# A fused retention and gated MLP kernel: states and cross products in 64-wide TensorE tiles, with the head halves of two of four pairs swapped

## The chip, the core and the metric

The kernel runs on one core of one Trainium2 chip. The metric is the time of one execution on the device in microseconds, as the median of several runs. The core has five engines that this text names as the profile does: PE (TensorE, the matrix unit), DVE (VectorE), ACT (ScalarE), POOL (GpSimd) and SP (SyncE, which issues the DMAs here). PE reads its operands from SBUF and writes into PSUM, which has eight banks of 512 fp32 columns; DVE and ACT carry results from PSUM back to SBUF. A PE matmul has a stationary operand (the weights, brought in by a separate weight load, "PEld" in the profile) and a moving operand.

## The reference

Eight batches, eight heads, 576 positions, head size 64. Each head does retention: scores decayed by a power of a head's gamma, and no softmax. The result is laid out as 4608 tokens of 512 features and goes through an MLP with a gate.

```
scores = q @ k.T / sqrt(64)
ret    = scores * gamma[h] ** (i - j)   for j <= i, else 0
attn   = ret @ v                        # (8, 8, 576, 64)
x      = attn.transpose(0, 2, 1, 3).reshape(4608, 512)
h      = x @ w_in                       # 512 x 2048
g      = h * sigmoid(beta * h)
out    = g @ w_out                      # 2048 x 512, fp32
```

## The kernel before, in words

**Retention by chunks.** Since the decay is a power of the distance, it is split into a factor on q (`gq`) and one on v (`gv`). The first 512 positions of a batch are four chunks of 128 keys (`c` = 0 to 3); the last 64 positions of two batches together make a "tail" block. `seq` lists all of them in order, and every helper takes an index `i` into it. The eight heads are four pairs `p`, the two heads `j` of a pair lying on the two halves of 64 partitions. For a chunk:

- `a_sc` (L320) makes scores: for each pair and each head a matmul of 64 rows of weights (`kT`), so that the two heads of a pair use the upper and the lower half of the array, each into a PSUM bank of its own. DVE multiplies them by the causal mask into `R`.
- `a_O` (L375) multiplies `R` by v: weights of 128 rows and 64 columns, so that the two heads of a pair write the two halves of the output's partitions.
- `a_st` (L404) adds k^T v of the chunk to a running state in PSUM: four matmuls, one per pair, each 128 x 128 with 128 moving columns. Of each 128 x 128 result only the two diagonal 64 x 64 blocks are wanted; two ACT copies (L419) carry them to a tile `sbd` (or `end`, after the last chunk), whose other two blocks were set to zero at the start (L155).
- `a_cross` (L356) adds what earlier chunks give: q times the state before this chunk, four matmuls per chunk (L372), each with a block-diagonal 128 x 128 `sbd` as weights and 128 moving columns, into the same PSUM bank as `a_O`'s. Tails use `ends` with 64 moving columns (L369).
- `a_x` (L390) copies the finished block from PSUM to `xT`, the transposed activations.

**The MLP.** `up` (L424) multiplies four slices `ko` of `w_in` (128 rows each, one per head pair) by `xT` with 512 moving columns and lets ACT apply the gate (L433) into `gT`; `down` (L457) multiplies `gT` by `w_out` (L464), and a copy and a DMA carry the result out. Both run in bf16 with 512 moving columns.

**The order of work** is written out by hand. `fill` is a list of up and down steps of all blocks, one after the other. `merged` (L484) emits them in order and, at numbered places, what the `streams` hold: loads, casts, transposes and the retention of the next batch. A batch from number 2 on has at one place `first` (L596: state of chunk 0, scores of chunks 0 and 1), two steps later the state of chunk 1, at a later place `first` again (state of chunk 2, scores of chunks 2 and 3), and five steps after that `outputs` (L601: all four `a_O`, the three crosses, the four copies, the state of chunk 3). Batches 0 and 1 are at the start and partly written out line by line (L498 to L593). Each engine runs its instructions in the order in which they are emitted.

**The start.** `w_in` arrives on SP's queue in seven pieces of columns (L165: six of 256 and one of 512) and is cast to bf16 by DVE and POOL (`cast_w_in`, L180), half of the 128-row slices each. Behind it come the four groups of `w_out`, into the same four staging buffers `wt`, and are cast and scaled by 1/beta (`cast_w_out`, L198): group 0 by DVE (three slices) and POOL (one), groups 1 to 3 by DVE and ACT. The first block's up steps run while the pieces arrive; its down steps start with the first two slices of `w_out` (`down_rows`, L551). Behind `w_out` the q, k and v of batch 1 are loaded.

Of the kernel before, what the change touches and what calls it, by code (L numbers as in the profile page):

```python
# [19 lines left out]
def kernel(  # L20
# [10 lines left out]
    nc = tc.nc  # L31
# [139 lines left out]
    def load_w_in(g):  # L171
        f0, fn = pieces[g]
        if f0 % 512 == 0:
            whole[0] = stage.tile([P, KO, 512], F32, name="wt", tag="wt", bufs=4)
        t = whole[0][:, :, f0 % 512:f0 % 512 + fn]
        for w in (slice(0, 2), slice(2, KO)) if g in (0, 1, NP - 1) else (slice(0, KO),):
            nc.sync.dma_start(t[:, w], w_in_r[:, w, f0:f0 + fn])  # L177
        wts[g] = t

    def cast_w_in(g, kos=range(KO)):  # L180
        t = wts[g]
        f0, fn = pieces[g]
        for ko in kos:
            on_pool = ko < 2 if g == 0 else ko % 2
            e = nc.gpsimd if on_pool else nc.vector
            if fn > 256 and ko == 2:
                for x in range(0, fn, 256):
                    for o, eng in ((2, nc.vector), (3, nc.gpsimd)):
                        eng.tensor_copy(w_in_sb[:, o, f0 + x:f0 + x + 256], t[:, o, x:x + 256])
            elif fn == 256 or ko < 2:  # L190
                e.tensor_copy(w_in_sb[:, ko, f0:f0 + fn], t[:, ko])  # L191

    def load_w_out(g):
        t = stage.tile([P, KO, d_model], F32, name="wt", tag="wt", bufs=4)
# [3 lines left out]
    def cast_w_out(g):  # L198
        t = wts.pop(NP + g)
        for i in range(KO):  # L200
            fo = g * KO + i
            if i == KO - 1 and g == 0:
                nc.gpsimd.tensor_tensor(w_out_sb[:, fo, :], t[:, i], rbeta_sb[:, fo:fo + 1].to_broadcast([P, d_model]), ALU.mult)
            elif i == KO - 1:
                nc.scalar.activation(w_out_sb[:, fo, :], t[:, i], ACT.Copy, scale=rbeta_sb[:, fo:fo + 1])
            else:
                nc.vector.tensor_scalar(w_out_sb[:, fo, :], t[:, i], rbeta_sb[:, fo:fo + 1], None, ALU.mult)  # L207
# [76 lines left out]
    def heads(t, p):  # L284
        return t[:, 2 * p:2 * p + 2, :].rearrange("p h d -> p (h d)")
# [63 lines left out]
    def O_of(i, p):  # L349
        Os = live[i]["O"]  # L350
        return Os[p // 2][:, p % 2] if split(i) else Os[0][:, p]

    def opens(i, p):
        return p == 0 or split(i) and p == 2

    def a_cross(i, first):  # L356

        b, c = seq[i]
        if first:
            new_O(i)  # L360
        if c == 0 and b is not None:
            return
        for p in range(HP):
            rhs, view = q_cols(i, slice(0, P), p)
            O = O_of(i, p)
            if b is None:
                for x in range(2):
                    r = slice(x * TL, (x + 1) * TL)
                    nc.tensor.matmul(O[:, r], ends[(2 * c + x) % 4][:, p, :], rhs[:, r],  # L369
                                     start=False, stop=True, skip_group_check=True)  # L370
            else:
                nc.tensor.matmul(view(O), sbds[(c - 1) % NS][:, p, :], rhs,  # L372
                                 start=first and opens(i, p), stop=not first, skip_group_check=True)

    def a_O(i):  # L375

        b, c = seq[i]
        L = live[i]

        early = i < E  # L380
        if not early:
            new_O(i)
        R, vn = L["R"], L["vn"]
        crossed = b is None or c > 0
        for j, p in [(n // HP, n % HP) if early else (n % 2, n // 2) for n in range(H)]:
            nc.tensor.matmul(O_of(i, p)[j * D:(j + 1) * D], vn[:, 2 * p + j, :], R[:, j, p, :],  # L386
                             start=opens(i, p) and not (early and crossed), stop=early or not crossed,
                             skip_group_check=True)

# [14 lines left out]
    def a_st(i):  # L404

        b, c = seq[i]
        if b is None:
            return
        L = live[i]
        if c == 0:  # L410
            state_ps[b] = psum.tile([P, HP, P], F32, name="st", tag="st", bufs=1)
        st = state_ps[b]
        for p in range(HP):
            nc.tensor.matmul(st[:, p, :], heads(L["kn"], p), heads(L["vn"], p),  # L414
                             start=(c == 0 and p == 0), stop=True, skip_group_check=True)
        s = ends[b % 4] if c == CB - 1 else sbds[c % NS]
        for j in range(2):
            r = slice(j * D, (j + 1) * D)
            (nc.vector.tensor_copy if i == CB + 2 else nc.scalar.copy)(s[r, :, j * D:(j + 1) * D], st[r, :, j * D:(j + 1) * D])  # L419


    gts = {}
# [71 lines left out]
    def F(f, *a):  # L494
        return lambda: f(*a)
# [76 lines left out]
    def second(i):  # L572
        for f in (a_O, lambda j: a_cross(j, False), a_x):
# [32 lines left out]

    def pair_prep(i, at):
        b, c = seq[i]
# [18 lines left out]
    for n in range(1, B - 1):  # L627

        take = [i for i in todo if seq[i][0] == n + 1 or n == B - 2 or seq[i] == (None, 0) and n == CB - 1]
        todo = todo[len(take):]  # L630
        lo, hi = (base[n] + 17, base[n + 1] - 9.5) if n == 1 else (base[n] + 3, base[n + 1] - 8)
        at = [lo + x * (hi - lo) / (len(take) - 1) for x in range(len(take))]
        if len(take) == 2 and n > 1:
            at[1] -= 6
        for i, t in zip(take, at):
            st = pair_prep(i, t) + [(t, F(first, i))]
            if seq[i][0] is None:
                st.append((t + 5, F(second, i)))
# [37 lines left out]
```

## Time and profile before

| what | value |
|---|---|
| median of three runs | 307.72 us (307.54 to 307.96) |
| the profiled execution's own time | 308.28 us |
| its span, first to last instruction | 306.6 us |
| granted PE clock | 1.0 throughout |
| PE busy / weight loads busy | 298.1 us (97%) / 155.8 us (51%) |
| DVE / ACT / POOL busy | 105.8 (35%) / 141.2 (46%) / 99.5 us (32%) |
| PE, 0 to 21.0 us | 15.97 us busy |
| PE, 21.0 to 34.2 us | 12.87 of 13.2 us busy |
| PE, 34.2 to 248 us | busy without a gap worth naming |
| HBM traffic | 36.71 MB read, 9.44 MB written |

The profiled execution took 1.68 us more than its span, and 0.56 us more than the median. Busy time of PE counts a matmul from its start to its modelled end, and matmuls overlap, so "97% busy" says that PE was seldom without work, not that it ran at its peak: what a matmul costs is read from the distance between starts. The chain of work that ended last, one of the views, gives these distances in groups: a start, a length, an engine with its tile and line, and how many instructions.

### The profile page before, as it was taken

What the parts mean: (1) busy time and instruction counts of PE and PEld (TensorE: products, weight loads), DVE (VectorE), ACT (ScalarE), POOL (GpSimd) and SP (SyncE); (2) the same over time, 40 slices, a digit from 0 to 9 for tenths busy, and PEclk for the clock granted to TensorE, in tenths of its full rate; (3) what the DMA queues carried; (4) which work ended last, traced back from release to release, by engine and by line L of the source; (5) the groups of instructions that cost most, each with busy time, mean ns of one, the idle gap of its engine ahead of it and who ended that gap; (6) DMA issues with size and microseconds to landing.
All of it is one profiled execution on the core that took longest, in us unless ns stands there. A gap on an engine that the chain in (4) does not pass through costs nothing.

```text
span 306.6 us, 5337 instructions
## 1 busy us (share of the span) xinstructions
PE 298.1 (97%) x2145; PEld 155.8 (51%) x2145; DVE 105.8 (35%) x192; ACT 141.2 (46%) x249; POOL 99.5 (32%) x136
## 2 busy tenths in 40 slices
PE   7789999999999999999999999999999999999996
PEld 5544456855554454454554545454545444444444
DVE  7554466504730433234430623053414420010012
ACT  5567546783148313660286208710773047207700
POOL 4666117653743264354326032812330000000000
PEclk9999999999999999999999999999999999999999
DMA  8999999999999999999994499939980110031012
GB/s 211 218 335 379 382 239 255 231 193 236 177 276 179 238 270 222 216 263 187 186 258 77 106 223 259 169 88 206 203 126 2 71 68 0 23 79 36 0 68 71
DMA packets 128697, 53.84 MB, mean 176 GB/s; under 512 B 109968, under 2 KB 121632, under 8 KB 128672
## 3 DMA queue, kind: packets, MB, share of 16 engines
q1 hardware_dynamic: 128640, 53.49, 79.9%
q8 instruction: 17, 0.28, 0.4%
q14 instruction: 8, 0.07, 0.1%
q10 hardware_dynamic: 32, 0.01, 0.0%
HBM read 36.71 MB, written 9.44 MB: 151 GB/s over the span
## 4 chain that ended last, share of the span: by engine, by line
PE 88%; DMA 5%; SPq 4%; DVE 1%; POOL 0%; issue 0%; DVEq 0%
PE po L464 41%; PE ph L431 36%; DMA wt<-in_moe_w_out_dram 3%; SPq L95 3%; PE sc L330 3%; PE O L386 3%; DMA wt<-in_moe_w_in_dram 2%; PE st L414 2%; PE O L372 2%; SPq L177 1%; DVE w_out_sb L207 1%; PE O L369 0%; SPq L83 0%; PE T L304 0%; PE T L310 0%
## 5 line engine op out<-in xcount | busy, mean ns | idle before, releaser
L433 ACT ACTIVATE gT<-ph,beta_sb 128x512 bf16<-128x512 f32 (+1 forms) x152 | 99.1, 659 | 82.6 <-PE ph L431 82.2
L464 PE MATMUL po<-w_out_sb,gT 128*128 128x512 bf16 (+2 forms) x608 | 129.2, 368 | 0.4 <-DVE w_out_sb L207 0.4
L431 PE MATMUL ph<-xT,w_in_sb 128*128 128x512 bf16 (+1 forms) x608 | 127.4, 365 | 0.0
L431 PEld LDWEIGHTS <-w_in_sb 128*128 128x128 bf16 x608 | 58.2, 98 | 61.6 <-DVE w_in_sb L191 0.7
L464 PEld LDWEIGHTS <-gT 128*128 128x128 bf16 x608 | 57.1, 98 | 63.1 <-issue 0.6
L335 DVE TENSOR_TENSOR R<-sc,causal 128x512 bf16<-128x512 f32 x72 | 45.0, 684 | 78.2 <-PE sc L330 77.1
L471 DVE COPY ot<-po 128x512 f32<-128x512 f32 (+2 forms) x34 | 22.4, 659 | 85.0 <-PE po L464 84.9
L262 POOL TENSOR_TENSOR vn<-kvn,gv 128x512 bf16<-128x512 f32 x32 | 33.2, 1042 | 19.8 <-PE O L386 9.6
L280 POOL CAST kn<-kvn 128x512 bf16<-128x512 f32 x32 | 19.6, 615 | 44.1 <-DMA kvn<-in_k_dram 39.2
L254 POOL TENSOR_TENSOR qs<-qn,gq 128x512 bf16<-128x512 f32 x24 | 24.3, 1042 | 28.1 <-DMA qn<-in_q_dram 28.1
L419 ACT CAST sbd<-st 64x256 bf16<-64x256 f32 x46 | 16.7, 363 | 18.8 <-PE st L414 18.2
L402 DVE CAST xT<-O 128x512 bf16<-128x512 f32 x24 | 15.7, 687 | 16.5 <-PE O L386 9.1
L402 ACT CAST xT<-O 128x512 bf16<-128x512 f32 x10 | 5.9, 587 | 30.9 <-PE O L372 30.9
L414 PE MATMUL st<-vn,kn 128*128 128x128 bf16 x128 | 12.4, 219 | 0.1
L414 PEld LDWEIGHTS <-kn 128*128 128x128 bf16 x128 | 9.2, 98 | 4.7
L330 PE MATMUL sc<-qT,kT 64*128 64x128 bf16 x256 | 10.8, 218 | 0.7 <-ACT kT L311 0.6
L386 PEld LDWEIGHTS <-vn 128*64 128x64 bf16 x288 | 8.5, 109 | 4.5 <-issue 3.6
L386 PE MATMUL O<-R,vn 128*64 128x128 bf16 x288 | 10.8, 221 | 0.0
L269 POOL TENSOR_TENSOR kn<-tln,gq 128x512 bf16<-128x512 f32 x4 | 4.2, 1042 | 19.4 <-DMA tln<-in_q_dram 19.4
L330 PEld LDWEIGHTS <-kT 64*128 64x128 bf16 x288 | 8.2, 94 | 4.5 <-issue 1.7
L191 POOL CAST w_in_sb<-wt 128x256 bf16<-128x256 f32 (+1 forms) x13 | 6.3, 508 | 5.0 <-DMA wt<-in_moe_w_in_dram 5.0
L215 PE MATMUL ph<-warm 128*128 128x128 f32 (+1 forms) x24 | 6.6, 409 | 1.2 <-DVE warm L120 1.2
(62 smaller groups left out, 92.4 us busy)
## 6 DMA issues: line engine op xcount, KB each, us to landing
qn<-in_q_dram SPq DMA_DIRECT2D x16, 512.0 KB, 5.4
kvn<-in_k_dram SPq DMA_DIRECT2D x32, 256.0 KB, 5.2
kvn<-in_v_dram SPq DMA_DIRECT2D x32, 256.0 KB, 5.1
out_dram<-ot SPq DMA_DIRECT2D x31, 256.0 KB, 3.0
wt<-in_moe_w_out_dram SPq DMA_DIRECT2D x4, 1024.0 KB, 10.0
wt<-in_moe_w_in_dram SPq DMA_DIRECT2D x6, 512.0 KB, 8.5
out_dram<-ot SPq DMA_DIRECT2D x9, 128.0 KB, 2.4
wt<-in_moe_w_in_dram SPq DMA_DIRECT2D x4, 256.0 KB, 6.3
```

The costliest lines, as they stand in the source:

```text
L254: e.tensor_tensor(batch[b]["qs"][:, cs, hs], q_tiles[b][:, hs, cs].rearrange("p h i d -> p i h d"), gq[:, cs, hs].unsqueeze(3).to_broadcas ...
L262: nc.gpsimd.tensor_tensor(live[i]["vn"][:], kv_tiles.pop(i)[:, 1], gains(gv, c), ALU.mult)
L280: nc.gpsimd.tensor_copy(kn[:, c % 2], t[:, 0])
L330: nc.tensor.matmul(view(sc[j][:, p, :]), L["kT"][r, p, :], rhs, start=True, stop=True, skip_group_check=True)
L335: nc.vector.tensor_tensor(R[:, j], sc[j][:], m_b, ALU.mult)
L386: nc.tensor.matmul(O_of(i, p)[j * D:(j + 1) * D], vn[:, 2 * p + j, :], R[:, j, p, :], start=opens(i, p) and not (early and crossed), stop= ...
L402: (nc.scalar.copy if on_act else nc.vector.tensor_copy)(x, view(Os[0]))
L414: nc.tensor.matmul(st[:, p, :], heads(L["kn"], p), heads(L["vn"], p), start=(c == 0 and p == 0), stop=True, skip_group_check=True)
L431: nc.tensor.matmul(ph, w_in_sb[:, ko, fo * P:(fo + 1) * P], xts[m][:, ko, :, w], start=(ko == 0), stop=(ko == KO - 1))
L433: nc.scalar.activation(gts[m][:, fo, :, w], ph, ACT.Silu, scale=beta_sb[:, fo:fo + 1])
L464: nc.tensor.matmul(po[:, :nn], gT[:, fo, ms, :], w_out_sb[:, fo, n0:n0 + nn], start=(fo == 0), stop=(fo == FO - 1))
L471: (nc.scalar.copy if m == 0 else nc.vector.tensor_copy)(ot, po[:, :nn])
```

## The change

- **States.** For batches from number 2 on (`b >= QB`), `a_st` makes a state by eight matmuls instead of four: per head, weights of 128 rows and 64 columns, 64 moving columns, the two heads of a pair into the two halves of the partitions. The state lies dense in PSUM, 64 columns per pair, and after chunks 0 to 2 one ACT copy of 128 x 256 takes it to a new tile `sbq`; after chunk 3 two copies take it to `ends` as before.
- **Cross products.** For these batches `crosses` replaces `a_cross`: per chunk eight matmuls of 64 rows and 64 columns with 128 moving columns. They go in groups of four that use the four 64 x 64 quarters of the array: upper rows to left columns, lower rows to right columns, and for a pair with a number two higher the other two.
- **Swapped halves.** So that the second two of the four can write the other half of the partitions, the two heads of pairs 2 and 3 change places everywhere behind the scores: in `a_O` (all batches), in `ends` and `sbds` (ten blocks of 64 columns now, L152), in `xT`, and in the rows of `w_in` of slices 2 and 3.
- **Output tiles.** `a_O4` puts two chunks and two pairs into one PSUM bank instead of one chunk and four pairs; `x4` copies the four banks to `xT`, three by DVE and one by ACT.
- **Order.** The state of chunk 1 moves from two steps behind the first `first` to the beginning of the second; the state of chunk 2 moves from there to the beginning of `outputs`, in front of the 32 matmuls of `a_O4`, and the state of chunk 3 from the end of `outputs` to between `a_O4` and `crosses`. `a_O` of batch 0 takes the heads of a pair in turn.
- **Casts of w_in.** All pieces have 256 columns (eight pieces). POOL casts slices 0 and 1 of each; DVE casts slices 2 and 3, each in two copies of 64 partitions that change places. The last piece's cast and the load of the last `w_out` group are two steps later (10.1 and 10.2). Of `w_out` group 0, POOL casts two slices instead of one and DVE two instead of three.

```diff
-    sbds = [consts.tile([P, HP, P], BF16, name=f"sbd{i}") for i in range(NS)]
-    ends = [consts.tile([P, HP, P], BF16, name=f"end{i}") for i in range(4)]
+    sbds = [consts.tile([P, 10, D], BF16, name=f"sbd{i}") for i in range(1)]
+    ends = [consts.tile([P, 10, D], BF16, name=f"end{i}") for i in range(4)]
+    sbq = [consts.tile([P, HP, D], BF16, name=f"sbq{i}") for i in range(NS)]
     for s in sbds + ends:
         nc.vector.memset(s[:], 0.0)
+    sbds += ends[2:]
...
-    pieces = [(f, 256) for f in range(0, 1536, 256)] + [(f, 512) for f in range(1536, d_ff, 512)]
+    pieces = [(f, 256) for f in range(0, d_ff, 256)]
...
-        for w in (slice(0, 2), slice(2, KO)) if g in (0, 1, NP - 1) else (slice(0, KO),):
+        for w in (slice(0, 2), slice(2, KO)) if g < 2 else (slice(0, KO),):
...
-    def cast_w_in(g, kos=range(KO)):
+    def cast_w_in(g):
         t = wts[g]
         f0, fn = pieces[g]
-        for ko in kos:
-            on_pool = ko < 2 if g == 0 else ko % 2
-            e = nc.gpsimd if on_pool else nc.vector
...
+        for ko in range(2):
+            nc.gpsimd.tensor_copy(w_in_sb[:, ko, f0:f0 + fn], t[:, ko])
+        for ko in range(2, KO):
+            for hh in range(2):
+                nc.vector.tensor_copy(w_in_sb[hh * D:(hh + 1) * D, ko, f0:f0 + fn], t[(1 - hh) * D:(2 - hh) * D, ko])
...
-            if i == KO - 1 and g == 0:
+            if i % 2 and g == 0:
                 nc.gpsimd.tensor_tensor(w_out_sb[:, fo, :], t[:, i], rbeta_sb[:, fo:fo + 1].to_broadcast([P, d_model]), ALU.mult)
...
+    def block(s, p):
+        f = 2 * p
+        return s[:, f:f + 2].rearrange("k h d -> k (h d)")
...
-        for j, p in [(n // HP, n % HP) if early else (n % 2, n // 2) for n in range(H)]:
-            nc.tensor.matmul(O_of(i, p)[j * D:(j + 1) * D], vn[:, 2 * p + j, :], R[:, j, p, :],
+        for hh, p in [(n % 2, n // 2) for n in range(H)]:
+            j = hh ^ p // 2
+            nc.tensor.matmul(O_of(i, p)[hh * D:(hh + 1) * D], vn[:, 2 * p + j, :], R[:, j, p, :],
...
-        st = state_ps[b]
+        st, tiled = state_ps[b], b >= QB
         for p in range(HP):
-            nc.tensor.matmul(st[:, p, :], heads(L["kn"], p), heads(L["vn"], p),
-                             start=(c == 0 and p == 0), stop=True, skip_group_check=True)
+            if tiled:
+                for j in range(2):
+                    nc.tensor.matmul(st[j * D:(j + 1) * D, p, :D], L["kn"][:, 2 * p + j, :], L["vn"][:, 2 * p + j, :],
+                                     start=(c == 0 and p == 0), stop=True, skip_group_check=True)
+            else:
+                nc.tensor.matmul(st[:, p, :], heads(L["kn"], p), heads(L["vn"], p),
+                                 start=(c == 0 and p == 0), stop=True, skip_group_check=True)
+        if tiled and c < CB - 1:
+            nc.scalar.copy(sbq[c % NS][:], st[:, :, :D])
+            return
         s = ends[b % 4] if c == CB - 1 else sbds[c % NS]
...
+    def crosses(i):
+
+        for c in range(1, CB):
+            for p, x in [(p, x) for p in range(2) for x in range(4)]:
+                r, hh, p = slice(x % 2 * D, x % 2 * D + D), x % 2 ^ x // 2, p + x // 2 * 2
+                rhs, _ = q_cols(i + c, r, p)
+                nc.tensor.matmul(out4(i + c, p, hh), sbq[c - 1][r, p, :], rhs, start=False, stop=True, skip_group_check=True)
+
+    def out4(i, p, hh):
+
+        c = seq[i][1]
+        return live[i - c]["O4"][c // 2, p // 2][hh * D:(hh + 1) * D, p % 2, :, c % 2 * PC:(c % 2 + 1) * PC]
+
+    def a_O4(i):
...
+        if c % 2 == 0:
+            for u in range(2):
+                live[i - c]["O4"][c // 2, u] = psum.tile([P, 2, CB, 2 * PC], F32, name="O", tag="sc" if c else "O", bufs=2)
+        for n in range(H):
+            hh, p = n % 2, n // 2
+            j = hh ^ p // 2
+            nc.tensor.matmul(out4(i, p, hh), L["vn"][:, 2 * p + j, :], L["R"][:, j, p, :].rearrange("k (i s) -> k i s", i=CB),
+                             start=c % 2 == 0 and p % 2 == 0, stop=False, skip_group_check=True)
+
+    def x4(i):
+
+        b = seq[i][0]
+        for c, u in ((0, 0), (0, 1), (1, 0), (1, 1)):
+            (nc.scalar.copy if (c, u) == (0, 1) else nc.vector.tensor_copy)(
+                xt(b)[:, 2 * u:2 * u + 2, :, 2 * c * PC:2 * (c + 1) * PC], live[i]["O4"][c, u][:])
...
-                (8.2, F(load_w_out, 3))],
+                (10.1, F(cast_w_in, 7)), (10.2, F(load_w_out, 3))],
...
     def first(i):
-        a_st(i)
+        a_st(i - (seq[i][1] == 2 and seq[i][0] is not None))
         a_sc(i)
         a_sc(i + 1)
 
     def outputs(i):
-        for f in (a_O, lambda j: a_cross(j, False), a_x):
-            for j in range(i, i + CB):
-                f(j)
-        a_st(i + CB - 1)
+        a_st(i + 2)
+        for j in range(i, i + CB):
+            a_O4(j)
+        a_st(i + 3)
+        crosses(i)
+        x4(i)
...
-            elif seq[i][1] == 0:
-                st.append((t + 2, F(a_st, i + 1)))
-            else:
+            elif seq[i][1] > 0:
                 st.append((t + 5, F(outputs, i - 2)))
```

More of the change, by code (lines that the diff above doesn't have):

```diff
@@ L175, in load_w_in @@
         t = whole[0][:, :, f0 % 512:f0 % 512 + fn]
-        for w in (slice(0, 2), slice(2, KO)) if g in (0, 1, NP - 1) else (slice(0, KO),):
+        for w in (slice(0, 2), slice(2, KO)) if g < 2 else (slice(0, KO),):
             nc.sync.dma_start(t[:, w], w_in_r[:, w, f0:f0 + fn])
         wts[g] = t
-    def cast_w_in(g, kos=range(KO)):
+    def cast_w_in(g):
         t = wts[g]
         f0, fn = pieces[g]
-        for ko in kos:
-            on_pool = ko < 2 if g == 0 else ko % 2
-            e = nc.gpsimd if on_pool else nc.vector
[L186 to L191, printed above, removed]
+        for ko in range(2):
[3 more added lines that the diff above has]
+                nc.vector.tensor_copy(w_in_sb[hh * D:(hh + 1) * D, ko, f0:f0 + fn], t[(1 - hh) * D:(2 - hh) * D, ko])
     def load_w_out(g):
@@ L368, in a_cross @@
                     r = slice(x * TL, (x + 1) * TL)
-                    nc.tensor.matmul(O[:, r], ends[(2 * c + x) % 4][:, p, :], rhs[:, r],
+                    nc.tensor.matmul(O[:, r], block(ends[(2 * c + x) % 4], p), rhs[:, r],
                                      start=False, stop=True, skip_group_check=True)
             else:
-                nc.tensor.matmul(view(O), sbds[(c - 1) % NS][:, p, :], rhs,
+                nc.tensor.matmul(view(O), block(sbds[(c - 1) % NS], p), rhs,
                                  start=first and opens(i, p), stop=not first, skip_group_check=True)
@@ L416, in a_st @@
+        if tiled and c < CB - 1:
+            nc.scalar.copy(sbq[c % NS][:], st[:, :, :D])
+            return
         s = ends[b % 4] if c == CB - 1 else sbds[c % NS]
         for j in range(2):
-            r = slice(j * D, (j + 1) * D)
-            (nc.vector.tensor_copy if i == CB + 2 else nc.scalar.copy)(s[r, :, j * D:(j + 1) * D], st[r, :, j * D:(j + 1) * D])
+            r, w = slice(j * D, (j + 1) * D), slice(0, D) if tiled else slice(j * D, (j + 1) * D)
+            (nc.vector.tensor_copy if i == CB + 2 else nc.scalar.copy)(
+                s[r, slice(1, 7) if j else slice(0, 10)].rearrange("k (u y) d -> k u y d", u=2)[:, :, 0:3:2], st[r, :, w].rearrange("k (u y) d -> k u y d", u=2))
@@ new lines, in a_O4 @@
+    def a_O4(i):
+        c, L = seq[i][1], live[i]
+        if c == 0:
+            L["O4"] = {}
+        if c % 2 == 0:
[6 more added lines that the diff above has]
+                             start=c % 2 == 0 and p % 2 == 0, stop=False, skip_group_check=True)
```

## The prediction

> **What bounds the kernel now.** I read the page's shares first, then the chain of waits in order of time, then the start as a timeline.
>
> ```profile
> PE 298.1 (97%) x2145; PEld 155.8 (51%) x2145; DVE 105.8 (35%) x192; ACT 141.2 (46%) x249; POOL 99.5 (32%) x136
> PE 88%; DMA 5%; SPq 4%; DVE 1%; POOL 0%; issue 0%; DVEq 0%
> ```
>
> PE is 88% of the chain; the DMA and SPq shares lie in the first 34 us. Behind that only a change in the spacing of PE's matmuls, or a new stall of PE, moves the time. One batch (number 4) with the tail before it, from the chain (start, length, what):
>
> ```profile
> 125.62 0.57 PE O L386 x16
> 126.19 0.57 PE O L369 x16
> 126.77 5.18 PE ph L431 x24
> 131.94 0.22 PE st L414 x4
> 132.17 0.55 PE sc L330 x16
> 132.72 1.83 PE ph L431 x8
> 134.55 0.22 PE st L414 x4
> 134.78 6.91 PE po L464 x32
> 141.68 0.22 PE st L414 x4
> 141.91 0.55 PE sc L330 x16
> 142.46 4.42 PE po L464 x20
> 146.88 1.01 PE O L386 x32
> 147.90 0.78 PE O L372 x12
> 148.68 0.22 PE st L414 x4
> ```
>
> Here is what a matmul costs in each shape. 24 ph in 5.18 us: 0.216 each. 4 st in 0.22: 0.0555. O x16 against x32 (0.57, 1.01): 0.444 for 16 more, so a pair on the two column halves takes 0.0555, with 0.12 once on entering. sc x8 takes 0.33 elsewhere in the chain and x16 0.55: 0.0555 per pair on the two row halves, 0.11 on entering. Crosses: 12 x 0.0555 = 0.67, so 0.11 for coming back from halves. 8 ph behind sc take 1.83 instead of 1.73: 0.10 for coming back. L369 has 64 moving columns: (0.57 - 0.11) / 16 = 0.0288 each. So a change of array shape costs 0.10 to 0.12, and a batch costs 0.22 + 0.55 + 0.10 + 0.22 + 0.22 + 0.55 + 0.10 + 1.01 + 0.78 + 0.22 = 3.97 us beside its up and down steps.
>
> The start, as a timeline:
>
> ```profile
> 22.52 0.69 DVE L191 CAST w_in_sb<-wt 128x256 bf16<-128x256 f32 x2 [1.06 <-DMA wt<-in_moe_w_in_dram]
> 22.55 0.92 POOL L191 CAST w_in_sb<-wt 128x256 bf16<-128x256 f32 x2 [0.28 <-DMA wt<-in_moe_w_in_dram]
> ...
> 32.52 2.06 DVE L207 TENSOR_SCALAR w_out_sb<-wt,rbeta_sb 128x512 bf16<-128x512 f32 x3 [2.08 <-DMA wt<-in_moe_w_out_dram]
> 32.56 1.34 POOL L203 TENSOR_TENSOR w_out_sb<-wt,rbeta_sb 128x512 bf16<-128x512 f32 x1 [1.87 <-DMA wt<-in_moe_w_out_dram]
> ...
> 34.23 10.09 PE L464 MATMUL po<-w_out_sb,gT 128*128 128x512 bf16 x46 [0.36 <-DVE w_out_sb L207]
> ```
>
> Casts wait for pieces of w_in, which land about every 1.5 us; PE's last wait, 0.36 us, is for the second slice of w_out, on which DVE lost time beside POOL (three casts in 2.06 us, against 1.28 for a later three).
>
> **Part 1: states and crosses, batches 2 to 7.** A state becomes eight matmuls in four column pairs with 64 moving columns. No row shows this shape. From above, it costs what it does now (pairs at 0.0555: 0.222); from below, pairs at L369's 0.0288: 0.115. The single records at 80.9 us speak for the lower: the first two pairs of 64-column weight loads of O start 0.029 us apart, and in the stream a load runs beside the matmul before it. I take 0.115. The crosses become 24 matmuls in six groups of four. From above, two at a time (0.666); from below, four in 0.0555 (0.333). Row pairs and column pairs each run whole side by side, their starts 0.003 us apart, and four quarters read no more than a column pair and write no more than a row pair, so I take 0.333. Changes between two split shapes are not in the trace either: between nothing and 0.12; I take 0.11, since going in and coming out cost that alike. After, each `first`: 0.12 in, 0.115 state, 0.11, 0.444 scores, 0.10 out = 0.89. `outputs`: 0.12, 0.115, 0.888, 0.115, 0.11, 0.333, 0.10 = 1.78. The batch: 2 x 0.89 + 1.78 = 3.56, so 0.41 less, and 6 x 0.41 = **2.45 us saved**.
>
> Bounds: with both upper prices a batch is 4 x 0.107 + 0.333 = 0.76 dearer than that, 4.32, or 2.1 us lost in six; with free changes between split shapes (three per batch) another 2.0 us is saved.
>
> A rule against this: the Trainium skill, "TensorE: Matmul & The Clock Gate", section on 56 instead of 53.3 ns, says that matmul starts never come closer than some 25 ns, however small. The 0.003 us between a pair's starts disagree with it as a rule for neighbours; as a mean no row here goes under 0.0277. By it the 56 small matmuls of a batch would take 1.4 us instead of 0.79, and part 1 would lose 1.2 us.
>
> **What the moved states wait for.** The state of chunk 3 now stands behind an ACT copy of the state of chunk 2, and behind it on PE are the crosses and the next down steps. In the trace that copy starts 0.256 us after the last st matmul (75.765, 76.021) and takes 0.366: some 0.65 with the signal. The 32 matmuls in between take 0.89, so it is covered by 0.24, as long as ACT is idle. All six `outputs` stand in or behind down steps (po rows before each), where ACT has no gate work; should a gate (0.687) be in front, the stall is up to 0.45 a batch. I put it at nothing. The state of chunk 1, two steps later, has its copy read only in `outputs`, five steps (over 4 us) on. `x4` makes four copies as before; the po copies queued behind them on DVE come every 3.45 us (16 matmuls), the three DVE copies take 2.06, so nothing waits. ACT loses 18 copies of 0.363, off the path.
>
> **Part 2: the start.** DVE gets four casts of 64 x 256 per piece instead of two of 128 x 256; a cast's time goes with its columns. Two now take 0.69 beside POOL; the extra two, POOL done, 0.21 to 0.29 each (0.209 is the spacing of the two at 19.52, 0.294 a whole one). So a piece's last slice is ready 0.4 to 0.6 later: 23.9 instead of 23.5 for the third piece. PE, which starts that matmul at 23.57 now, is then 0.4 late, and no later for the rest, since 1.4 us of DVE per piece stays under PE's 1.73. From above: two casts held by POOL's two like the slowest here (0.49) and two whole ones (0.294) make 1.57 per piece against landings every 1.50, 0.5 more by the eighth, some 1.2 us lost with w_out's part below; from below nothing. Halving the 512 piece makes its megabyte land in 2 x 1.50 instead of 2 x 1.36 us (landings at 25.53, 27.02, 28.38, 29.74), so w_out comes 0.28 later. Its slices: the second, on POOL, 32.56 + 0.28 + 1.34 = 34.18, about where DVE has it now; the fourth, POOL's second, 1.04 to 1.34 on, 35.2 to 35.5, where PE wants it at 35.1. PE's 0.4 is thus eaten by the 0.36 wait, and what is left is 0.15 to 0.45: **0.3 lost**. The load of the fourth w_out group, two steps later on SP, is issued at about 31.3 instead of 30.7, with q and k behind it; they land behind queued transfers (q at 42.1) and nothing comes later. SP issues ten w_in loads, as now.
>
> The rest costs nothing: five memsets for seven and batch 0's heads in turn lie in the first 19 us, before the first piece of w_in lands (18.8); `ends` in ten blocks keeps the copies' 256 columns.
>
> **Sum.** -2.45 + 0.3 = -2.15. The profiled execution, 308.28, would come to 306.1; it was 0.56 over the median, so 307.72 - 2.15 = **305.6 us**.
>
> **Rivals.**
> - *Small matmuls don't start closer than now* (0.0277 each: slower). Place: the 56 small matmuls of a batch. Price: both upper bounds, +2.1 + 0.3 = +2.4: 310.1. It decides from a mean of 0.0206 on, where 6 x 56 x (0.0206 - 0.0142) eats the 2.15. For it: no row has a denser mean. Against: PE's sequencer passes the eight instructions between two of its waits in 0.125 us (67.663, 67.788), and 33 instructions are still to start when it reaches the closing drain at 302.36, so a short burst is stocked.
> - *Loads of 64-column weights set the pace of the states*: no gain there, +2.57 on the forecast: 308.1, about the same. Against: the 0.029 above.
> - *Only two of the four crosses run at once*, because two row halves write one bank: +2.0: 307.6, the same. The scores, which run side by side, write two banks, so no row excludes it. The Trainium skill, "TensorEngine Tiling (Array Packing)", Gotcha 1, says that different row tiles cannot access the same PSUM bank at one time; in the first two of each four they do, on different partitions. By that rule the sum would be -0.15 instead of -2.15, and no run here shows yet which holds.
> - *DVE is late at the start*: 1.2 instead of 0.3: 306.5.
> - *The change doesn't do what it says* can't be: the built order of instructions has the new shapes, 336 PE instructions more.
>
> **Chances.** Forecast 0.66 (its own range 304.6 to 306.6: changes of shape a little cheaper, or the start 1.2 late), small matmuls no denser 0.12, states without gain 0.08, crosses two at a time 0.08, late start 0.06. About 0.2% (0.62 us) is what a measurement can tell from no change. Faster: 0.66 + 0.06 = 0.72. The two cases near zero give 0.12 to "same" and 0.04 to "slower", with the 0.12 of the first rival 0.16. The range leaves out the first rival and 0.05 below: 304.3, toward free changes of shape, to 308.9, past the two cases near zero.
>
> **What would show it.** In the chain after: st x8 near 0.12 beside its entry, O x32 0.89 right behind it, 24 crosses near 0.45 with entry; 3.56 per batch. The first rival is right if the crosses take 0.67 or more. At the start: DVE casts of 64 partitions in fours, near 1.4 us per piece, and PE's wait for w_out at 34 to 35.5. A PE wait for ACT before the state of chunk 3, or for DVE at `a_O4`, would prove the covers wrong.

## The result, and the profile after

| | median, us | lowest to highest | ratio to before, 95% interval |
|---|---|---|---|
| before | 307.77 | 307.29 to 308.43 | |
| changed | 306.61 | 305.58 to 307.50 | 0.9959 [0.9947, 0.9971] |

The change saves 1.16 us where 2.15 was forecast. It is faster, as forecast, and inside the range, but half of the gain is missing. The median lies at the upper edge of the forecast's own range (306.6), which was set for a late start. The profiled execution of the changed kernel took 306.56 us with a span of 304.8.

The page of the changed kernel, its PE row and the shares of the chain of waits by engine:

```profile
PE 294.4 (97%) x2279; PEld 152.0 (50%) x2313; DVE 110.3 (36%) x206; ACT 135.8 (45%) x231; POOL 99.6 (33%) x138
PE 74%; SPq 10%; DMA 10%; issue 2%; POOL 2%; DVE 1%; ACT 0%; POOLq 0%
```

PE had 88% of the chain and has 74%; the DMA and SyncE's queue (SPq) have 20%. Before, their share lay in the first 34 us. Now the chain leaves PE in the middle of the run. Here is the chain around batch 4 (start, length, what):

```profile
120.43 6.00 DMA kvn<-in_v_dram
...
126.56 1.05 POOL vn L260
127.62 0.63 SPq L286
...
129.53 5.66 DMA kvn<-in_k_dram
135.19 6.20 DMA kT<-kn
141.39 0.05 issue
141.44 0.62 PE sc L328 x16
142.06 0.16 issue
142.22 4.26 PE po L510 x19
146.48 0.25 PE st L419 x8
146.73 0.90 PE O L457 x32
147.62 0.12 PE st L419 x8
```

The scores of batch 4's second pair (chunks 2 and 3) start when the transpose of its keys lands, at 141.39, and what the chain shows ahead of it are the loads and transposes that stand before it in SyncE's queue. The waits of the changed kernel (engine, line, releaser: total, times, longest) give the price:

```profile
PEld L328 <- DMA kT<-kn: 1.0, 1, 1.0
PE sc L328 <- DMA kT<-kn: 0.9, 1, 0.9
```

One wait of some 1.0 us, which the kernel before does not have. There the same transpose landed at 140.07, and the scores started at 141.84, 1.77 us later: this distance is called the slack below. (The 0.16 "issue" in the chain is no loss: one matmul record is missing there.)

What PE does is as forecast, nearly. In another execution of the changed kernel (run `e8_changed_again` below), which has no wait in this batch, the chain reads:

```profile
139.89 0.24 PE st L419 x8
140.13 0.55 PE sc L328 x16
140.69 4.42 PE po L510 x20
145.11 0.24 PE st L419 x8
145.36 0.90 PE O L457 x32
146.25 0.12 PE st L419 x8
146.38 0.46 PE O L439 x24
146.84 0.97 PE po L510 x4
```

Eight 64-column state matmuls take 0.12 us (0.24 where the change of shape is theirs), the 32 O matmuls 0.90 right behind them, 24 cross products 0.46 with their entry. Counted from the last full matmul ahead to the first behind, less the 0.216 that one takes anyway, each stretch of scores costs 0.893 (0.872 before), the stretch of outputs 1.820 (2.014 before), and the lone state of chunk 1, 0.223, is gone. A batch costs 3.61 instead of 3.98.

The start of the profiled execution of the changed kernel, as a timeline:

```profile
20.25 1.30 DVE L189 CAST w_in_sb<-wt 64x256 bf16<-64x256 f32 x4 [0.66 <-DMA wt<-in_moe_w_in_dram]
...
32.06 2.51 POOL L201 TENSOR_TENSOR w_out_sb<-wt,rbeta_sb 128x512 bf16<-128x512 f32 x2 [1.99 <-DMA wt<-in_moe_w_out_dram]
...
33.13 10.72 PE L510 MATMUL po<-w_out_sb,gT 128*128 128x512 bf16 x47
43.69 0.61 PE L302 MATMUL T<-ident,qs 128*128 128x128 bf16 x8
```

Batch 1's first transpose starts at 43.69 here and at 44.16 before, so this start looks 0.47 us faster. It isn't: the loads were earlier in this execution. Seen from the landing of w_in's second piece (20.22 here, 20.98 before), the transpose is at 23.47 instead of 23.18, 0.29 later.

Two distances thus tell the runs apart without the luck of the loads: from the landing of w_in's second piece to batch 1's first transpose (the start), and from that transpose to the last matmul (the rest). The runs e1 to e11 are the experiments below:

| kernel | start, us | rest, us | median of the times, us |
|---|---|---|---|
| before | 23.18 | 259.13 | 307.6 to 307.8 |
| e2: before, keys sooner | 23.18 | 259.13 | 307.62 |
| e10: before, last piece halved | 23.49 | 259.13 | 308.08 |
| e4: swap only | 23.46 | 259.13 | 308.23 |
| changed | 23.47 | 257.93 | 306.61 |
| e8: changed again | 23.48 | 256.93 | 306.26 |
| e1: changed, keys sooner | 24.27 | 256.94 | 305.58 |
| e11: e1 again | 23.48 | 256.94 | 305.55 |
| e3: e1, quarters in two halves | 23.46 | 257.77 | 306.48 |
| e5: e1, states whole | 23.47 | 258.57 | 307.17 |
| e6: e1, casts on ACT too | 23.47 | 256.94 | 305.82 |
| e9: e6, last piece whole | 23.35 | 256.93 | 305.09 |

(In e1's execution the fourth load of output weights landed 0.9 late and PE waited for it, hence 24.27. e7 is not listed, because its profiled execution ran at a granted clock of 0.853, where the others had 0.999 or 1.0.) The rest is the same to 0.01 us wherever PE does the same work without a wait: 259.13 before, 256.93 after, so the matmuls save **2.20 us**. The start costs **0.29**. The profiled execution of the changed kernel has 257.93, the wait of **1.00**. Together with the loads, 0.76 earlier: -2.20 + 1.00 + 0.29 - 0.76 = -1.67, and the two chains end at 303.53 and 301.87, 1.66 apart.

### The profile page after: what moved, and what is told of

Same layout as the page of the kernel before. It is cut to its first block, busy times and chain, and to the rows that moved or that the text cites. A ratio compares the mean times of both kernels' runs of the same rounds, so it can differ in the third digit from the quotient of the medians.

```text
span 304.8 us, 5634 instructions
## 1 busy us (share of the span) xinstructions
PE 294.4 (97%) x2279; PEld 152.0 (50%) x2313; DVE 110.3 (36%) x206; ACT 135.8 (45%) x231; POOL 99.6 (33%) x138
## 4 chain that ended last, share of the span: by engine, by line
PE 74%; SPq 10%; DMA 10%; issue 2%; POOL 2%; DVE 1%; ACT 0%; POOLq 0%
PE po L510 34%; PE ph L477 32%; SPq L95 4%; SPq L109 3%; PE sc L328 2%; DMA qn<-in_q_dram 2%; DMA kT<-kn 2%; DMA wt<-in_moe_w_in_dram 2%; DMA kvn<-in_v_dram 2%; DMA kvn<-in_k_dram 2%; PE O L457 1%; PE st L419 1%; SPq L83 1%; SPq L286 1%; SPq L501 1%
## 5 line engine op out<-in xcount | busy, mean ns | idle before, releaser
L510 PE MATMUL po<-w_out_sb,gT 128*128 128x512 bf16 (+2 forms) x590 | 126.6, 368 | 1.9 <-issue 1.3
L477 PE MATMUL ph<-xT,w_in_sb 128*128 128x512 bf16 (+1 forms) x593 | 125.9, 365 | 1.0 <-DVE w_in_sb L189 0.2
L260 POOL TENSOR_TENSOR vn<-kvn,gv 128x512 bf16<-128x512 f32 x32 | 33.4, 1044 | 19.8 <-DMA kvn<-in_v_dram 10.1
L425 ACT CAST sbq<-st 128x256 bf16<-128x256 f32 x18 | 6.7, 370 | 44.1 <-PE st L419 44.1
L464 DVE CAST xT<-O 128x512 bf16<-128x512 f32 x18 | 11.3, 684 | 15.6 <-PE O L439 15.6
L189 DVE CAST w_in_sb<-wt 64x256 bf16<-64x256 f32 x32 | 10.9, 340 | 1.4 <-DMA wt<-in_moe_w_in_dram 0.7
L430 ACT CAST end<-st 64x256 bf16<-64x256 f32 x22 | 8.1, 367 | 5.2 <-PE st L419 3.7
L419 PEld LDWEIGHTS <-kn 128*64 128x64 bf16 x192 | 5.1, 111 | 7.6 <-issue 6.8
L186 POOL CAST w_in_sb<-wt 128x256 bf16<-128x256 f32 x16 | 6.3, 424 | 6.2 <-DMA wt<-in_moe_w_in_dram 6.2
L419 PE MATMUL st<-vn,kn 128*64 128x64 bf16 x192 | 7.4, 200 | 0.1
L205 DVE TENSOR_SCALAR w_out_sb<-wt,rbeta_sb 128x512 bf16<-128x512 f32 x11 | 5.5, 553 | 5.0 <-DMA wt<-in_moe_w_out_dram 5.0
```

The costliest lines, as they stand in the source:

```text
L260: nc.gpsimd.tensor_tensor(live[i]["vn"][:], kv_tiles.pop(i)[:, 1], gains(gv, c), ALU.mult)
L419: nc.tensor.matmul(st[j * D:(j + 1) * D, p, :D], L["kn"][:, 2 * p + j, :], L["vn"][:, 2 * p + j, :], start=(c == 0 and p == 0), stop=True, ...
L464: (nc.scalar.copy if (c, u) == (0, 1) else nc.vector.tensor_copy)(xt(b)[:, 2 * u:2 * u + 2, :, 2 * c * PC:2 * (c + 1) * PC], live[i]["O4"] ...
L477: nc.tensor.matmul(ph, w_in_sb[:, ko, fo * P:(fo + 1) * P], xts[m][:, ko, :, w], start=(ko == 0), stop=(ko == KO - 1))
L510: nc.tensor.matmul(po[:, :nn], gT[:, fo, ms, :], w_out_sb[:, fo, n0:n0 + nn], start=(fo == 0), stop=(fo == FO - 1))
```

## The experiments

### Is the missing microsecond the wait for keys?

Batch 4's second pair of keys is cast and transposed ahead of batch 5's loads in SyncE's order, in the changed kernel (e1) and in the one before (e2):

```diff
+        soon = b == XB + 2 and c > 0
-        return st + [(at - (25.4 if early else 28), F(load_kv, n)), (at - (25.3 if early else 26), F(load_kv, n + 1)), (at - 16, F(pre, i)),
-                     (at - 15, F(pre, i + 1)), (at - 10.5, F(x_k, b, c // 2))]
+        return st + [(at - (25.4 if early else 28), F(load_kv, n)), (at - (25.3 if early else 26), F(load_kv, n + 1)), (at - (20.7 if soon else 16), F(pre, i)),
+                     (at - (20.6 if soon else 15), F(pre, i + 1)), (at - (20 if soon else 10.5), F(x_k, b, c // 2))]
```

> The changed kernel, with one transpose of keys (batch 4, second pair) and the casts that feed it put ahead of batch 5's loads of queries, keys and values in SP's order. Theory (the PE gain is whole, 2.2 us, and 1.0 us of it is lost where scores of batch 4 wait for that transpose): the wait goes, the time is 306.6 - 1.0 = 305.6 us. Rival 1 (the load chain as a whole is the bound there, the wait only moves to batch 5): 306.4 to 306.8. Rival 2 (the missing 1 us was lost at the start and the wait is one profiled execution's accident): 306.6.

> The kernel before with the same transpose moved ahead in the same way. Theory (there the transpose landed 1.77 us ahead of its scores, so nothing waits for it): no change, 307.8 us. Rival (TensorE lost time to the load chain before the change too): about 307.0.

Measured: e1 305.58 us (305.45 to 306.03; ratio to before 0.9930 [0.9909, 0.9952]), e2 307.62 (0.9999 [0.9986, 1.0012]). The chain of e1:

```profile
133.81 6.91 PE po L510 x32
140.72 0.24 PE st L419 x8
140.96 0.55 PE sc L328 x16
```

PE runs through; the transpose now lands at 130.94, ten microseconds ahead, and no later wait takes the place of the one removed. So the wait costs the changed kernel about 1 us of its median (306.61 - 305.58, from two sets of runs, so roughly), and the kernel before has nothing to gain there. Rival 1, a load chain that binds as a whole, is out, and so is a loss at the start (rival 2).

The changed kernel and e1 were each run once more, to see whether the wait is there every time:

> The changed kernel itself once more, on the same chip as the next three, as their base beside the kernel with the keys turned sooner. Theory (the wait of scores for keys of batch 4 costs 0.7 to 1.0 us, as much as the start runs ahead of the loads): 306.4 to 306.7 us, and in its trace the wait stands again, at about 140 us. Rival (the wait was one execution's accident): no wait in the trace, and 305.6.

> The changed kernel with the keys turned sooner once more, as the base of the run with the last piece whole on the same chip: 305.6 to 305.8 us, and no wait for keys in batch 4 in its trace.

Measured: e8 306.26 us median, single runs from 305.16 to 306.91 (0.9951 [0.9934, 0.9967]); e11 305.55, from 305.25 to 305.79 (0.9936 [0.9923, 0.9948]). The expectation of e8 was half wrong: its time is near, but its profiled execution, the fastest of the changed kernel, has no wait. The transpose landed at 138.38 and the scores started at 140.07. So the wait comes in some executions and not in others; in how many, two traces can't say. That it makes the wide spread of the changed kernel's times (1.9 us in twelve runs, 1.75 in e8's six) is not shown: e1, e11, e6 and e9, each run four or five times, spread over 0.5 to 0.7 us, but e3, in which the transpose is moved too, over 2.4 us in twelve. In the traces the wait follows from single transfers that land 0.6 to 1.9 us later than the distance of their neighbours. They stand in every trace, some in nearly the same place (the one at 81 us), others not. In the first profiled execution of the changed kernel two hit this chain: a load of values at 126.43 (2.36 us behind the one ahead of it, where 1.2 is usual) and the transpose itself at 141.39 (2.27 behind the load ahead). In e8 neither came. With the slack of 1.69 us that e8 shows, the changed kernel bears one late transfer, by estimate, and not two. The kernel before had one in this chain, a load of values at 137.14, and still 1.77 us left, some 3.2 without it.

The slack itself differs from execution to execution. In e4 and e10 (below) PE keeps the pace of the kernel before, and the transpose landed at 140.92 and 140.72, only 0.51 and 0.61 us ahead of the scores. That is less than the 0.91 us by which the changed PE comes sooner there. So the 1.77 of the one trace of before was not a safe figure, and by estimate PE in the changed kernel would have waited in both of these.

### What does the swap cost at the start?

The swapped halves, the casts and the loads alone. States and cross products are those of the kernel before: `outputs`, the lone state of chunk 1 and the three `sbds` are put back too.

```diff
...
-        st, tiled = state_ps[b], b >= QB
+        st, tiled = state_ps[b], False
...
-        a_st(i - (seq[i][1] == 2 and seq[i][0] is not None))
+        a_st(i)
...
```

> The changed kernel's second part alone: swapped halves of the head pairs, w_in cast by VectorE in halves with the swap, w_in's loads of the third piece in two, POOL's slices of w_out; states and cross products are 128 columns wide in their old places. It prices the start. Forecast on record: +0.3 us (0 to 1.2), 308.07 us. Reading of the two traces (output weights' landing to the first down product is the same within 0.02 us): no change, 307.8 us. If the start gained what the two profiled executions differ by, 0.47 us: 307.3.

Measured: 308.23 us, 1.0018 [1.0005, 1.0031], so 0.15 to 0.95 us slower. The forecast, 0.3, lies in it (the piece that is loaded in two is the last one, not the third as the expectation says); my reading of the two traces ("no change"), made from the landing of the output weights, was wrong, because the halved loads move that landing too. The start distance, 23.46 instead of 23.18, gives 0.28, and the rest is 259.13, so the swapped heads cost nothing later.

Two things can make up the 0.28: DVE's four casts of the second piece, or the output weights, which land later behind the halved last piece. First, ScalarE takes two of those four casts (e6):

```diff
-                nc.vector.tensor_copy(w_in_sb[hh * D:(hh + 1) * D, ko, f0:f0 + fn], t[(1 - hh) * D:(2 - hh) * D, ko])
+                (nc.scalar.copy if g == 1 and ko == 3 else nc.vector.tensor_copy)(
+                    w_in_sb[hh * D:(hh + 1) * D, ko, f0:f0 + fn], t[(1 - hh) * D:(2 - hh) * D, ko])
```

> The changed kernel with the keys turned sooner (305.6 us), and of the four VectorE casts of w_in's second piece two put on ScalarE. Theory (behind the second piece's landing the changed kernel's TensorE runs without a break, so its four casts of 1.31 us set the start, and the start is 0.28 us later than before, seen from that landing): 0.2 to 0.3 us less, 305.3. Rival (the output weights, which land 0.27 us later, set it as much): no change, 305.6.

Measured: 305.82 us (0.9935 [0.9922, 0.9948]), start 23.47: no change, as the rival says. The chain of e6 shows what stands behind the casts, equally long:

```profile
22.49 9.77 DMA wt<-in_moe_w_out_dram
...
32.40 2.52 POOL w_out_sb L202 x2
34.92 0.04 issue
34.96 9.22 PE po L511 x42
```

POOL's second slice of the output weights is ready at 34.92, and PE waits for it. Second, in the kernel before, the last piece of w_in is loaded and cast in halves; with it go, as in the change, the later places of its cast and of the load of the last `w_out` group, and nothing else is changed (e10):

```diff
-    pieces = [(f, 256) for f in range(0, 1536, 256)] + [(f, 512) for f in range(1536, d_ff, 512)]
+    pieces = [(f, 256) for f in range(0, d_ff, 256)]
...
-        for w in (slice(0, 2), slice(2, KO)) if g in (0, 1, NP - 1) else (slice(0, KO),):
+        for w in (slice(0, 2), slice(2, KO)) if g < 2 else (slice(0, KO),):
...
-                (8.2, F(load_w_out, 3))],
+                (10.1, F(cast_w_in, 7)), (10.2, F(load_w_out, 3))],
```

> The kernel before, with w_in's last piece alone loaded and cast in two column halves. Theory (1 KB rows in place of 2 KB bring the output weights 0.27 us later, and TensorE waits for them there): first transpose of batch 1 23.2 us after w_in's second piece lands in place of 22.96, and 308.0 us. Rival (the wait for the output weights hides it): 22.96 and 307.7.

Measured: 308.08 us, 1.0015 [1.0006, 1.0025], start 23.49 (the expectations of e9 and e10 count to the last matmul ahead of the transpose, 0.22 us sooner, so 23.27 against 22.96). The halves alone cost all of it: the output weights land 11.75 us behind the second piece instead of 11.44, and in the chain of e10 they are what PE waits for:

```profile
22.10 9.81 DMA wt<-in_moe_w_out_dram
...
32.00 1.68 DVE w_out_sb L207 x2
33.68 0.04 issue
33.72 10.09 PE po L464 x46
43.81 0.45 PE T L304 x8
```

Third, both are put right in e6: the last piece whole, cast by 256 columns, and one slice of the output weights on POOL (e9):

```diff
-    pieces = [(f, 256) for f in range(0, d_ff, 256)]
+    pieces = [(f, 256) for f in range(0, 1536, 256)] + [(f, 512) for f in range(1536, d_ff, 512)]
...
+        for x in range(0, fn, 256):
...
-            if i % 2 and g == 0:
+            if i == KO - 1 and g == 0:
...
```

> The run with ScalarE casts (305.8 us), and besides w_in's last piece loaded as before, by rows of 512 columns in two loads, and one slice of w_out on POOL in place of two, as before. Theory (the start's 0.28 us lies in two chains of equal length, four casts of the second piece, and the output weights that land 0.27 us later with two slices in a row on POOL; with both gone TensorE is as early as before): first transpose of batch 1 22.96 us after w_in's second piece lands, as before, in place of 23.25, and 305.4 us. Rival (a third chain as long, such as the eight VectorE casts of the last piece): 23.2 or more, 305.7.

Measured: 305.09 us (304.98 to 305.52; 0.9923 [0.9909, 0.9936]), the lowest median of the set, 0.46 under e11 on the same chip, though the intervals overlap. Its start distance, 23.35 (23.13 in the count of the expectation), lies between the two readings, 0.13 under e11's, and that alone is shown as the gain: in the profiled executions (304.98 and 305.79) most of the rest is w_in's second piece, which landed 0.70 sooner in e9. Its chain has no wait for weights left: PE runs without a break from batch 0 on, so its own work and no longer a landing sets this start.

```profile
18.50 1.24 PE ph L495 x5
19.74 0.02 issue
19.76 0.82 PE ph L495 x3
20.58 12.15 PE ph L480 x56
32.73 8.20 PE po L513 x38
```

### Do four quarters run at once?

The cross products of e1 in another order, first all that use two of the quarters, then all that use the other two:

```diff
-        for c in range(1, CB):
-            for p, x in [(p, x) for p in range(2) for x in range(4)]:
+        for half in range(2):
+            for c, p, x in [(c, p, 2 * half + y) for c in range(1, CB) for p in range(2) for y in range(2)]:
```

> The first kernel of this set with the order of the 24 cross products changed alone: first the twelve that use two of the quarters of the array, then the twelve that use the other two, so that the quarters can run only two at a time, but for one place in the middle. Theory (four quarters at once, a group every 0.0555 us): 11 groups in place of 6 in a batch, 5 x 0.0555 = 0.28 us more, times 6 batches = 1.67 us: 305.6 + 1.7 = 307.3 us. Rival (pairs only in any order, by the rule on row tiles that share a bank): the same as the first kernel of this set.

Measured: 306.48 us (0.9971 [0.9952, 0.9991]), 0.9 above e1; the rest is 257.77, 0.83 more. Half the expected loss, so both readings missed. The chain shows 0.60 instead of 0.46 for the 24:

```profile
146.98 0.12 PE st L419 x8
147.11 0.60 PE O L439 x24
```

The single records of another batch tell why (start in us behind 173, pairs of matmuls; the records don't name the quarter, and I sorted them into the two rows by their spacing):

```
first two quarters   .261 .341 .397 .453 .509 .564
other two quarters                  .406 .486 .542 .598 .654 .709
```

Read so, each quarter takes its next product every 0.0555 us (the second after 0.080), but the other two start when only three pairs of the first six have started: a product whose quarter is free does not wait for those ahead of it. The records bear the sorting out. Four of the 24 products raise a semaphore, each the last one into one of the four output banks, so the 4th, 12th, 16th and 24th as the program has them. In order of start, the marked records are the 4th, 12th, 18th and 24th, in all six batches, at .344, .489, .568 and .713 here: PE did not start them in the order of the program, and the rows above fit, with the 16th product at .489 ahead of the 9th to 12th. That some order costs more shows that order decides how many quarters work at a time; that four do is seen in e1 itself, where starts of four lie within 0.011 us and the fours follow each other every 0.0555 (the second after 0.080).

A second test keeps two quarters only, those on the diagonal, by leaving the swap out altogether (e7; w_in is loaded and cast as before):

```diff
...
-            j = hh ^ p // 2
+            j = hh
...
-            for p, x in [(p, x) for p in range(2) for x in range(4)]:
-                r, hh, p = slice(x % 2 * D, x % 2 * D + D), x % 2 ^ x // 2, p + x // 2 * 2
+            for p, hh in [(p, x) for p in range(HP) for x in range(2)]:
+                r = slice(hh * D, (hh + 1) * D)
...
```

> The changed kernel with the keys turned sooner (305.6 us), but heads not swapped: w_in is loaded and cast as in the kernel before, states are in 64-column tiles, and the cross products use two quarters of the array only, those on the diagonal. Theory (a quarter takes a cross product every 0.0555 us, whatever the others do): 12 rounds in place of 6, 6 x 6 x 0.0555 = 2.0 us more, less 0.28 at the start: 307.3. Rival (the swap brings nothing, as the sequencer sets the pace of small matmuls): 305.3.

Measured: 307.26 us (0.9988 [0.9974, 1.0002]), 1.69 over e1 and e11, where 2.0 - 0.28 = 1.7 was expected; there is the time alone to show it. Without the swap the change would not be told from the kernel before.

### What do states in 64-column tiles bring?

e1 with states of 128 columns at the changed places:

```diff
-                for j in range(2):
-                    nc.tensor.matmul(st[j * D:(j + 1) * D, p, :D], L["kn"][:, 2 * p + j, :], L["vn"][:, 2 * p + j, :],
+            nc.tensor.matmul(st[:, p, :], heads(L["kn"], p), heads(L["vn"], p),
...
-            nc.scalar.copy(sbq[c % NS][:], st[:, :, :D])
+            nc.scalar.copy(sbq[c % NS][:D], st[:D, :, :D])
+            nc.vector.tensor_copy(sbq[c % NS][D:], st[D:, :, D:])
```

> The changed kernel with the keys turned sooner (305.6 us), its states 128 columns wide again, four matmuls at the changed places; cross products stay in quarters. Theory (what 64-column states save is in part a change of shape): in the stretch of outputs two states cost 2 x (0.222 - 0.127) = 0.19 us more and one more return and entry 0.11; each of the two stretches of scores costs 0.02 less; 0.26 a batch, 6 x 0.26 = 1.55 us: 307.1. Rival (only the state's own matmuls count, four a batch): 6 x 4 x 0.095 = 2.3: 307.9. If states in column tiles are worth nothing: 305.6.

Measured: 307.17 us (0.9984 [0.9974, 0.9994]); the rest is 258.57, 1.63 more than in e1, and 1.55 was expected.

```profile
145.86 0.22 PE st L417 x4
146.08 1.01 PE O L453 x32
147.10 0.33 PE st L417 x4
147.43 0.46 PE O L435 x24
```

A state between O and crosses costs 0.33 instead of 0.12. Half of that difference is the change of shape: the four matmuls themselves are 0.22. In the stretches of scores 128-column states are even 0.02 cheaper (0.872 against 0.893), since a full-width state needs no entry.

## Why the prediction was right, and by how much it was off

- **What bounds the kernel: right at the start, incomplete behind it.** "Behind that only a change in the spacing of PE's matmuls, or a new stall of PE, moves the time" held, and such a stall came. The forecast looked for stalls at ScalarE's copies, at VectorE's and in the loads of the start only.
- **The failed step** is that the sum has no term for a wait for a DMA behind the start. The one sentence on later landings, "they land behind queued transfers (q at 42.1) and nothing comes later", is on the loads of the start, and the loads and transposes of the later batches are passed over. These had little room to come sooner with PE: from 58 to 148 us the DMA engines' busy share, as the profile counts it (it can pass 1) in stretches of 6 us, was 1.04 to 1.35 in the kernel before and 0.95 to 1.44 in the changed one. By the second scores of batch 4 PE comes 0.91 us sooner behind batch 1's first transpose (96.77 us in e8 instead of 97.68), and the slack of the transpose of keys, 1.77 us in the trace of before, could have been read there; so could the fact that one late transfer was already in it. In its place the runs show a wait of up to 1.0 us that one moved transpose takes away (e1).
- **Part 1: right in mechanism, 2.20 instead of 2.45.** Groups of four crosses come every 0.0555, as taken, but for the first, behind which the next comes after 0.080. A stretch of scores costs 0.893, as taken (0.89); the stretch of outputs costs 1.820 instead of 1.78, of which the crosses with the way back to the full shape make 0.462 instead of 0.433 (start to start, in e8). A pair of state matmuls starts 0.032 behind the last instead of 0.0288 (0.127 a state for 0.115), which the changes of shape around it nearly make up. A batch is 3.61 instead of 3.56, and the batch before is 3.98 instead of 3.97; six times the difference of the two is the missing 0.25.
- **The moved states: right.** No execution shows PE waiting for ScalarE's copy ahead of the state of chunk 3.
- **Part 2: right, 0.29 for 0.3**, and for the reason given: the casts' delay goes into the wait for the output weights, and what is left is that these land later behind the second piece, by 0.26 in the changed kernel and 0.31 in e10, where nothing else was changed and the start costs 0.31. POOL's second slice ends just when PE wants it (e6).
- **Sum.** -2.20 + 0.29 = -1.91; e1 and e11, the changed kernel without the wait, measured -2.01 and -2.17 against before (by their intervals, -1.5 to -2.8 and -1.6 to -2.4). The wait takes 0.7 to 1.0 of the median, or 0.5 to 0.9 by the ratios to before.
- **Rivals.** *Small matmuls don't start closer* and *weight loads set the pace* are out: 24 crosses take 0.33 us behind their entry, a mean of 0.0139, and pairs of state matmuls, each matmul with a weight load of its own, come every 0.032. The rule of some 25 ns in the Trainium skill, "TensorE: Matmul & The Clock Gate", section on 56 instead of 53.3 ns, would make the crosses 0.6 by estimate. *Only two of four at once* is out too: the first two of each four use different row tiles and write one PSUM bank, on different partitions, 0.003 us apart. So Gotcha 1 of the Trainium skill's "TensorEngine Tiling (Array Packing)", that different row tiles cannot access the same PSUM bank at one time, does not hold for this case. By the first rule the prediction had part 1 lose 1.2 us, by the second a sum of -0.15; the measurement decides. *DVE late at the start* is out (23.47 against 23.18), though its time, 306.5, is nearly the measured 306.61: the time alone could not have told it from the wait. The rival that came, a DMA that takes the gain back, was not on the list.

## What to carry to other kernels

When an engine on the critical path gets faster, read from the trace of before, for each transfer that it will meet, how long ahead it lands, and take away from that what the engine gains up to there: the smallest remainder, less a late transfer or two, says where the gain stops. One trace gives the slack of one execution only: here it was 0.51 to 1.77 us in three executions at the same pace of PE. Compare starts from a landing, not from zero, since the loads of two executions can differ by more than the change. Small matmuls in row and column tiles pay when neighbours share their shape: here the state between O and crosses saved about as much by sparing a change of shape as by its own columns (0.11 and 0.10), while a state ahead of scores saved nothing.

## What the runs showed of the hardware that I had not expected

- Quarters of the array run on their own: each took a product of 64 rows and 64 columns of weights with 128 moving columns every 0.0555 us, and matmuls for free quarters started ahead of earlier ones whose quarters were busy, three pairs deep (e3).
- Single transfers land 0.6 to 1.9 us later than their neighbours' distance, several in every execution, in places that partly differ from run to run (before: 81.4, 137.1, 151.2 us; changed: 81.1, 126.4, 141.4; e8: 80.8 and none between 94 and 131). What delays them was not tried and stays open.
- A megabyte of w_in in rows of 1 KB took 2.97 us, in rows of 2 KB 2.72 (landings in the changed kernel and before), and that alone was 0.3 us of the kernel's time (e10).
